# Block means of v beside the first two slots of v by engine copies, beside the others by smaller transfers, in a rearranged order of work

## The chip, the cores and the metric

The kernel runs on one core of a Trainium2 chip. A core has five engines with a queue each: TensorE (PE in the profile; PEld is its weight loads), VectorE (DVE), ScalarE (ACT), GpSimd (POOL) and SyncE (SP), which here only issues transfers. Transfers from every queue share the core's 16 DMA engines. The metric is the time on the device in microseconds, the median of several runs.

## The reference

The kernel computes an attention and behind it two feed-forward layers:

```python
k_sum = k.reshape(B, H, nb, block, D).max(axis=3)      # block = 32
v_sum = v.reshape(B, H, nb, block, D).mean(axis=3)
scores_l = scale * q k^T, kept where |i - j| < 16
scores_s = scale * q k_sum^T + log(block)
a = softmax(concat(scores_l, scores_s))
x = a @ concat(v, v_sum)                                # 1536 tokens x 512
g = relu(x @ w_in) ** 2;            x = g @ w_out       # 512 -> 2048 -> 512
h = x @ w_in2;  g = h * sigmoid(1.702 h);  out = g @ w_out2
```

There are 2 batches, 8 heads, 768 positions and a head size of 64, all in fp32. So each position attends to its near neighbours and to 24 block summaries of its batch.

## The kernel before

**Tiling.** The 1536 tokens are 12 blocks of 128 (`i`, six a batch), 6 units of 256 (`u`), and 3 token tiles of 512. A block is computed in two halves of 64 queries (`c`). Each half attends to a window of 96 neighbouring keys and to the 24 summaries, 120 rows together (`NK`). For the product with v the tile `vw_all` holds, for each of four slots (`NV`, block `i` uses slot `i % 4`) and each half, those 120 rows: the 96 rows of the window come from HBM (`load_vw`, one transfer a half), the 24 rows of the block means come from the tile `vs`.

**The steps.** The string `ORDER` lists them: `k`, `q` load a unit (the last figure tells whether it is packed: one transfer with 512-byte pieces, or two with 256-byte ones), `tk`, `tq` transpose it on PE and copy it out of PSUM, `pk` puts the maxima of k beside the keys of a unit. `sv` (`sum_v`) loads the three v units of a batch into the buffers of k, sums them with a matmul against `band` and copies the means to `vs` in four pieces. `ps` (`put_vs`) puts `vs` into the slots. `v` loads the windows. `h,i,e` (`head`) computes the scores of a block (with `e` 0), and for the four even or odd heads the exponentials on ACT (L559), their sum's small addition on POOL or DVE (L563) and the normalisation (L566). `t,i` (`tail`) transposes the probabilities (L587), copies them to `pT`, multiplies with `vw` (L599: 32 matmuls) and writes the result to `xh` and `xl`, a high and a low part of fp32. `w,f,z` (`prep`, `fetch`) loads a piece of 512 KB of a first-layer weight for one of the 16 slices `f` (z is 0 for `w_in`, 1 for `w_out`) and splits it into parts with ACT (L684, L715) and DVE (L688, L691, L720). `s,f,half` and `S,f` (`part`, `step`) do a slice of the first layer for the first token tile: `S` for all 512 tokens, `s` for 256 of them, so that `s,f,0` needs only the blocks 0 and 1. The products are L753 and L805. Steps of the first layer so begin while attention still runs, and the rest of both layers follows.

**What sets the order.** A planner (`Plan`) takes the steps as the string lists them, gives each operation a start on its engine by fixed costs, and may place a later step in an earlier gap. `soonest` picks the engine that would end first. At the end all instructions are issued in the order of the planned starts, so each engine runs its own list strictly in that order on the chip. Into planned gaps of PE up to the first product L805, `fill` puts matmuls on `ident` (L1108, `warm`) that compute nothing. A transfer issued on POOL (`dma_pool`) is planned to end with a fixed `LAND` after its bytes have moved.

In the kernel before, `put_vs` is two transfers a batch, issued by POOL, one for each half, each copying `vs` into all four slots (L421). Every block's L599 waits for them.

Of the kernel before, what the change touches and what calls it, by code (L numbers as in the profile page):

```python
# [24 lines left out]


ORDER = """
    sel k,1,1 m,0 k,0,1 m,1 k,2,1 tk,0 q,0,1 tk,1 q,1,1 tk,2 pk,2 tq,0 v,0 pk,0 h,1,0 tq,1 m,2 h,1,1 pk,1
    q,3,0 q,2,1 h,0,0 w,1,0 v,1 sv,0 h,3,0 h,0,1 k,3,0 tq,3 ps,0 w,1,1 t,1 h,2,0 v,2 h,2,1 t,0 h,3,1 s,1,0
    v,3 tq,2 tk,3 t,2 h,5,0 t,3 s,1,1 h,4,0 w,3,0 k,4,1 w,3,1 w,5,0 tk,4 s,3,0 w,5,1 s,3,1 w,0,0 k,5,0 S,5  # L30
    w,2,0 tk,5 w,9,0 h,5,1 v,4 pk,3 v,5 h,4,1 pk,4 w,0,1 s,0,0 h,7,0 t,5 w,7,0 w,2,1 s,0,1 sv,1 s,2,0 v,6
    w,9,1 S,9 w,4,0 t,4 w,4,1 s,2,1 h,6,0 q,4,1 w,6,0 S,4 w,6,1 w,7,1 tq,4 S,7 S,6 v,7 w,11,0 w,8,0 ps,1
    w,11,1 h,6,1 h,7,1 h,8,0 S,11 q,5,0 w,8,1 w,10,0 t,7 S,8 w,15,0 v,8 tq,5 h,9,0 t,6 v,9 w,10,1 w,13,0
    w,13,1 S,10 w,15,1 h,8,1 pk,5 w,12,0 t,8 S,13 w,14,0 w,14,1 v,10 h,10,0 S,15 h,9,1 w,12,1 t,9 v,11
    h,11,0 S,14 h,10,1 S,12 h,11,1 t,10 t,11
"""


# [74 lines left out]
class Plan:  # L113
# [8 lines left out]
    ISSUE = 0.5  # L122
    FLIGHT = 1.1
    LAND = 0.95
    lean = 0.5, 0.5

    def __init__(self):
# [19 lines left out]
    def op(self, eng, dur, fn, reads=(), writes=(), after=(), port=False, moves=0.0):  # L147
        ready = self._ready(eng, self._deps(reads, writes, after))
        assert not any(b.dead for b, _ in (*reads, *writes))
        o = Op()  # L150
        o.eng, o.fn, o.seq, o.far = eng, fn, len(self.ops), eng == "SP"
        if eng == "SP":
            o.start = self._place(("SP",), max(ready, 0.8), self.ISSUE)
            self._take("SP", o.start, self.ISSUE)
            t = self._place(("DMA",), o.start + self.FLIGHT, moves)
            if t > o.start + self.FLIGHT:
                self.busy["SP"].remove((o.start, o.start + self.ISSUE))
                o.start = self._place(("SP",), t - self.FLIGHT, self.ISSUE)
                self._take("SP", o.start, self.ISSUE)
                t = self._place(("DMA",), o.start + self.FLIGHT, moves)  # L160
            self._take("DMA", t, moves)
            o.end = t + moves + self.LAND
        else:
            lines = (eng, "PORT") if port else (eng,)
            o.start = self._place(lines, ready, dur)
            for e in lines:
                self._take(e, o.start, dur)
            o.end = o.start + dur
        self.ops.append(o)
        for b, key in reads:  # L170
            b.ops.append(o)
            b.readers.setdefault(key, []).append(o)
        for b, key in writes:
            b.ops.append(o)
            b.writer[key] = o
            b.readers[key] = []
        return o
# [7 lines left out]
    def dma_pool(self, moves, fn, reads=(), writes=()):  # L185

        o = self.op("POOL", 1.0, fn, reads, writes)
        t = self._place(("DMA",), o.end + 0.5, moves)
        self._take("DMA", t, moves)
        o.end, o.far = t + moves + self.LAND, True  # L190
        return o

    def soonest(self, choices, reads=(), writes=(), after=()):
# [61 lines left out]
def kernel(  # L255
# [11 lines left out]
    nc = tc.nc  # L267
    B, H, S, D = q.shape
# [5 lines left out]
    WIN = HALF + 2 * EDGE  # L274
    NSUM = S // BLK
    NK = WIN + NSUM
    NPAIR = H // 2
    NB = S // P
# [11 lines left out]
    NV = 4  # L290
# [13 lines left out]
    plan = Plan()  # L304
# [29 lines left out]
    def make_mask(i):  # L334
        mk = masks[i]
        nc.gpsimd.memset(mk, 0.0)
        for c in range(2):
            w0 = NSUM * (1 - c)
            rows = slice(c * HALF, (c + 1) * HALF)
            part = mk[rows, w0:w0 + WIN]  # L340
            nc.gpsimd.affine_select(out=part, in_=part, pattern=[[1, WIN]], compare_op=ALU.is_ge,
                                    fill=NEG, base=-1, channel_multiplier=-1)
            nc.gpsimd.affine_select(out=part, in_=part, pattern=[[-1, WIN]], compare_op=ALU.is_ge,
                                    fill=NEG, base=2 * EDGE - 1, channel_multiplier=1)
            s0 = 0 if c == 0 else WIN
            nc.gpsimd.memset(mk[rows, s0:s0 + NSUM], LOGB)
        if i == 1:
            nc.gpsimd.memset(mk[0:HALF, NSUM:NSUM + EDGE], NEG)
        if i == 2:
            nc.gpsimd.memset(mk[HALF:P, WIN - EDGE:WIN], NEG)  # L350
# [14 lines left out]
    vw_all = attn.tile([NK, NV, 2, H * D], F32, tag="vw", name="vw")  # L365
    vw_ring = Ring(NV, lambda i: vw_all[:, i])
    vs_of = {}
    vs_rows = [Buf([], None) for _ in range(NV)]
# [5 lines left out]
    kin, qin, qT, kw, ks, vw, vs = {}, {}, {}, {}, {}, {}, {}  # L374
# [39 lines left out]
        vw[i] = buf  # L414

    def put_vs(b):
        for n in range(NV):
            vs_of[n] = b
        for c in range(2):
            r0 = 0 if c == 0 else WIN  # L420
            plan.dma_pool(0.5, lambda c=c, r0=r0: nc.gpsimd.dma_start(  # L421
                out=vw_all[r0:r0 + NSUM, :, c, :], in_=vs[b].t.unsqueeze(1).to_broadcast([NSUM, NV, H * D])),
                reads=[(vs[b], p) for p in range(NPAIR)], writes=[(vs_rows[n], c) for n in range(NV)])

    def sum_v(b):
        ps = banks.take()
# [299 lines left out]
    def prep(m, f, n=None, zs=(0, 1)):  # L726
        for z in zs:
            if z == 0:
                w_sb[m, f] = [None] * 4
            w_sb[m, f][2 * z:2 * z + 2] = hi, lo = [  # L730
                wt.hold() if n is None else wt.named(4 * n + 2 * z + i) for i in range(2)]
            parts(fetch(m, f, z), ALL, hi, ALL, lo, ALL)
# [323 lines left out]
    def part(f, h0, h1):  # L1056
        count = [x + (h0 <= h < h1) for h, x in enumerate(steps)]
        step(0, 0, f, h0 * HT, h1 * HT, [x == 1 for x in count], [x == NF for x in count])
        steps[:] = count

    todo = dict(
        k=load_k, q=load_q, v=load_vw, tk=t_k, tq=t_q,
        h=head, t=tail, ps=put_vs, pk=put_ks, sv=sum_v, w=lambda f, z: prep(0, f, f % RING, (z,)),
        m=lambda i: op("POOL", 1.6, lambda: make_mask(i), writes=[(consts, ("mask", i))]),
        s=lambda f, hf: part(f, hf, hf + 1),
        S=lambda f: part(f, 0, 2),
        sel=lambda: op("POOL", 1.3, make_band, writes=[(consts, "band")]),
# [74 lines left out]
```

## Time and profile before

| | |
|---|---|
| median of 3 runs | 592.22 us (591.78 to 593.14) |
| profiled execution | 593.77 us |
| its span, first to last instruction | 591.8 us |
| PE busy | 572.3 us (97%) |
| DVE busy | 477.4 us (81%) |
| ACT busy | 441.0 us (75%) |
| POOL busy | 65.4 us (11%) |
| moved by DMA | 96.19 MB, 163 GB/s |

Busy time is that of the whole span. It mixes the front, where loads and softmax feed PE, with the long layers behind it, and says little about either. Of use are the stretches of the span, the waits, and the chain of waits that ended last. The profile's line numbers are those of the kernel before; in the changed kernel the lines up to `put_vs` stand 1 further down and those behind it 15.

### The profile page before, as it was taken

The page shows a single profiled execution, that of the slowest core. Times are in us where ns is not written, and L with a number is a line of the kernel's source. Part 1 is how long each engine was busy: PE and PEld are TensorE (multiplying, and loading weights), DVE is VectorE, ACT ScalarE, POOL GpSimd, SP SyncE. Part 2 cuts the span into 40 slices and gives each one's busy share as a digit, 9 for nine tenths or more (in the row PEclk, how much of TensorE's full clock was granted, in tenths as well). Part 3 has the DMA queues.
Part 4 walks back from the last instruction along what each step waited for, and adds up shares of the span by engine and source line. Part 5 has one row for each costly group of instructions (what it writes and reads, how often), then busy time and mean ns, then how long its engine had stood idle before and what let it go on. Part 6 is the DMA issues. An engine that isn't in the chain of part 4 may idle for free.

```text
span 591.8 us, 9749 instructions
## 1 busy us (share of the span) xinstructions
PE 572.3 (97%) x3418; PEld 474.3 (80%) x3418; DVE 477.4 (81%) x1033; ACT 441.0 (75%) x908; POOL 65.4 (11%) x125
## 2 busy tenths in 40 slices
PE   7849999999999999999999999999999999999997
PEld 6648888888888888788888888888878888888885
DVE  4848998888889999889887799899998898877421
ACT  6958988988797768888778876776488777777322
POOL 5123414011200000110000001000100002000000
PEclk9979999999999999999999999999999999999999
DMA  9994999875345552455443536634355555556001
GB/s 227 251 247 101 252 272 237 229 202 171 107 143 178 179 177 73 145 153 182 151 140 119 174 123 207 211 109 140 115 172 161 186 173 164 171 179 210 2 0 72
DMA packets 87633, 96.19 MB, mean 163 GB/s; under 512 B 29536, under 2 KB 74592, under 8 KB 87584
## 3 DMA queue, kind: packets, MB, share of 16 engines
q1 hardware_dynamic: 87264, 94.78, 54.0%
q0 software_dynamic: 320, 0.79, 0.7%
q8 instruction: 27, 0.44, 0.3%
q14 instruction: 22, 0.18, 0.1%
HBM read 91.62 MB, written 3.15 MB: 160 GB/s over the span
## 4 chain that ended last, share of the span: by engine, by line
PE 88%; DMA 4%; DVE 3%; SPq 2%; ACT 1%; issue 1%; POOL 0%; DVEq 0%; POOLq 0%; ACTq 0%
PE acc L805 14%; PE acc L981 13%; PE acc L807 11%; PE m L981 10%; PE m L807 9%; PE h L753 8%; PE m L805 6%; PE acc L753 4%; PE h L981 4%; PE h L807 3%; PE m L753 2%; PE h L805 2%; DMA vw<-vs 2%; PE m L599 1%; DMA kin<-in_v_dram 1%; DMA qin<-in_q_dram 1%
## 5 line engine op out<-in xcount | busy, mean ns | idle before, releaser
L720 DVE TENSOR_TENSOR w<-xw,w 128x512 fp32r<-128x512 f32 (+1 forms) x167 | 111.3, 677 | 6.4 <-ACT w L715 3.5
L715 ACT CAST w<-xw 128x512 fp32r<-128x512 f32 (+1 forms) x164 | 96.9, 601 | 23.1 <-DVE xw L691 16.5
L691 DVE SCALAR_TENSOR_TENSOR xw<-raw,xw 128x512 uint32<-128x512 uint32 x148 | 101.3, 690 | 6.8 <-ACT raw L684 2.5
L684 ACT ACTIVATE raw<-raw 128x512 f32<-128x512 f32 x148 | 96.5, 674 | 9.6 <-DMA raw<-in_moe_w_in_dram 7.1
L805 PE MATMUL acc<-gh,w 128*128 128x512 f32 (+1 forms) x288 | 81.9, 369 | 0.0
L688 DVE TENSOR_SCALAR xw<-raw 128x512 uint32<-128x512 uint32 x148 | 64.0, 437 | 5.8 <-DMA raw<-in_moe_w_out_dram 3.8
L805 PEld LDWEIGHTS acc<-gh,w 128*128 128x128 f32 x288 | 51.7, 188 | 9.1 <-ACT sm L559 0.2
L807 PE MATMUL acc<-w,gh 128*128 128x512 f32 x184 | 56.7, 389 | 0.0
L753 PE MATMUL h<-xh,w 128*128 128x512 f32 (+1 forms) x184 | 55.1, 363 | 0.6 <-DVE r L769 0.5
L805 PE MATMUL acc<-gl,w 128*128 128x512 f32 (+1 forms) x144 | 52.8, 367 | 0.0
L807 PE MATMUL m<-w,gh 128*128 128x512 f32 x156 | 48.2, 390 | 0.0
L981 PE MATMUL acc<-top,w 128*128 128x512 f32 x186 | 47.4, 393 | 0.0
L715 ACT CAST gh<-gs 128x512 fp32r<-128x512 f32 x32 | 19.9, 622 | 35.5 <-PE h L807 25.4
L720 DVE TENSOR_TENSOR gl<-gs,gh 128x512 fp32r<-128x512 f32 x32 | 22.1, 691 | 28.5 <-ACT gh L715 27.9
L981 PEld LDWEIGHTS acc<-top,w 128*128 128x128 f32 x186 | 34.5, 188 | 8.9 <-ACT r L308 1.7
L807 PEld LDWEIGHTS acc<-w,gh 128*128 128x128 f32 x184 | 34.5, 188 | 7.2
L720 POOL TENSOR_TENSOR w<-xw,w 128x512 fp32r<-128x512 f32 x13 | 17.5, 1346 | 194.4 <-ACT w L715 182.5
L753 PEld LDWEIGHTS h<-xh,w 128*128 128x128 f32 x184 | 33.1, 188 | 6.5 <-DVE r L769 0.8
L559 ACT ACTIVATE sm<-sm,st 128x120 f32<-128x120 f32 x96 | 36.6, 383 | 0.0
L807 PE MATMUL acc<-w,gl 128*128 128x512 f32 x92 | 35.8, 389 | 0.0
L981 PE MATMUL m<-top,w 128*128 128x512 f32 x138 | 35.3, 391 | 0.0
L807 PEld LDWEIGHTS m<-w,gh 128*128 128x128 f32 x156 | 29.2, 188 | 6.3 <-ACT gh L782 0.4
(191 smaller groups left out, 1219.0 us busy)
## 6 DMA issues: line engine op xcount, KB each, us to landing
raw<-in_moe_w_out_dram SPq DMA_DIRECT2D x88, 512.0 KB, 3.5
raw<-in_moe_w_in_dram SPq DMA_DIRECT2D x60, 512.0 KB, 3.9
vw<-in_v_dram SPq DMA_DIRECT2D x20, 192.0 KB, 5.8
kin<-in_v_dram SPq DMA_DIRECT2D x6, 512.0 KB, 7.1
out_dram<-r SPq DMA_DIRECT2D x12, 256.0 KB, 2.1
kin<-in_k_dram SPq DMA_DIRECT2D x4, 512.0 KB, 6.1
qin<-in_q_dram SPq DMA_DIRECT2D x4, 512.0 KB, 7.2
qin<-in_q_dram SPq DMA_DIRECT2D x4, 256.0 KB, 4.8
```

The costliest lines, as they stand in the source:

```text
L559: nc.scalar.activation(out=s.t[:, h, :], in_=s.t[:, h, :], func=AF.Exp, bias=st.t[:, 0, h:h + 1], scale=-1.0, accum_out=st.t[:, 1, h:h + 1])
L599: nc.tensor.matmul(ps.t[e * D:(e + 1) * D, p * P + c * HALF:p * P + (c + 1) * HALF], lhsT=vw[i].t[:, c, h * D:(h + 1) * D], rhs=t.t[:, h, ...
L684: nc.scalar.activation(out=top, in_=top, func=AF.Prelu, scale=-(2.0 ** -80), alpha=-(2.0 ** -32))
L688: op("DVE", 0.36, lambda: nc.vector.tensor_scalar(out=x.t, in0=raw.t[:, :, 0], scalar1=29, scalar2=None, op0=ALU.logical_shift_right), rea ...
L691: op("DVE", 0.64, lambda: nc.vector.scalar_tensor_tensor(out=x.t, in0=raw.t[:, :, 1], scalar=3, in1=x.t, op0=ALU.logical_shift_left, op1=A ...
L715: plan.soonest([("ACT", 0.09 + 0.44 * fr, False, lambda: nc.scalar.copy(out=hi.t[:, hc], in_=src())), ("DVE", 0.05 + 0.4 * fr, True, lambd ...
L720: eng.tensor_tensor(out=lo.t[:, lc], in0=src(), in1=hi.t[:, hc].bitcast(F32), op=ALU.subtract)
L753: nc.tensor.matmul(hp.t[:, cols], lhsT=w.t[:, kc * P:(kc + 1) * P], rhs=x.t[:, kc, cols], start=(kc == 0 and n == 0), stop=(kc == KC - 1 a ...
L805: nc.tensor.matmul(a.t[:, cols], lhsT=w.t[:, j * P:(j + 1) * P], rhs=g.t[:, cols], **st)
L807: nc.tensor.matmul(a.t, lhsT=g.t[:, j * P:(j + 1) * P], rhs=w.t, **st)
L981: nc.tensor.matmul(bank.t, lhsT=a, rhs=rhs(b, kh), start=(begin and k == 0 and n == 0), stop=(k == 1 and n == 2), skip_group_check=True)
```

## The change

For each batch `put_vs` now does two things. For the first two slots that the batch uses (`near`: slots 0 and 1 in the first batch, 2 and 3 in the second) it copies `vs` with an engine, slot by slot and half by half, so four copies of 24x512, each on whichever of POOL, ACT and DVE the planner finds free soonest. For the other two slots POOL issues two transfers of half the size. In the plan a transfer of POOL is now taken to end 4 us later (`BEHIND`). And `ORDER` is another list, with the same steps.

```diff
 ORDER = """
-    sel k,1,1 m,0 k,0,1 m,1 k,2,1 tk,0 q,0,1 tk,1 q,1,1 tk,2 pk,2 tq,0 v,0 pk,0 h,1,0 tq,1 m,2 h,1,1 pk,1
+    m,1 k,2,1 sel w,1,0 m,0 k,1,1 q,1,1 k,0,1 tk,0 tk,1 tk,2 pk,0 q,0,1 sv,0 tq,0 h,1,0 tq,1 m,2 h,1,1 h,0,0
...
     LAND = 0.95
+    BEHIND = 4.0
...
-        o.end, o.far = t + moves + self.LAND, True
+        o.end, o.far = t + moves + self.LAND + self.BEHIND, True
...
     def put_vs(b):
+        near = (b * NB) % NV
+        for n in (near, near + 1):
+            for c in range(2):
+                r0 = 0 if c == 0 else WIN
+
+                def go(eng, n=n, c=c, r0=r0):
+                    (eng.copy if eng is nc.scalar else eng.tensor_copy)(
+                        out=vw_all[r0:r0 + NSUM, n, c, :], in_=vs[b].t)
+
+                plan.soonest([("POOL", 1.1, True, lambda go=go: go(nc.gpsimd)),
+                              ("ACT", 0.6, False, lambda go=go: go(nc.scalar)),
+                              ("DVE", 0.5, True, lambda go=go: go(nc.vector))],
+                             reads=[(vs[b], p) for p in range(NPAIR)], writes=[(vs_rows[n], c)])
+        far = NV - 2 - near
+        for c in range(2):
+            r0 = 0 if c == 0 else WIN
+            plan.dma_pool(0.6, lambda c=c, r0=r0: nc.gpsimd.dma_start(
+                out=vw_all[r0:r0 + NSUM, far:far + 2, c, :], in_=vs[b].t.unsqueeze(1).to_broadcast([NSUM, 2, H * D])),
+                reads=[(vs[b], p) for p in range(NPAIR)], writes=[(vs_rows[n], c) for n in (far, far + 1)])
         for n in range(NV):
             vs_of[n] = b
-        for c in range(2):
-            r0 = 0 if c == 0 else WIN
-            plan.dma_pool(0.5, lambda c=c, r0=r0: nc.gpsimd.dma_start(
-                out=vw_all[r0:r0 + NSUM, :, c, :], in_=vs[b].t.unsqueeze(1).to_broadcast([NSUM, NV, H * D])),
-                reads=[(vs[b], p) for p in range(NPAIR)], writes=[(vs_rows[n], c) for n in range(NV)])
```

What this moves is seen in three lists. The first is SP's, whose transfers start in this order, near the start of the program. In the kernel before, from its fourth load on (`qin` a q unit, `kin` a k unit, or a v unit where it is read from `in_v_dram`, `vw` a window of v, `raw` a weight piece; `x2` two alike):

```order
L380 DMA qin_152<-in_q_dram 128x8x128
L380 DMA qin_173<-in_q_dram 128x8x128
L411 DMA vw<-in_v_dram 80x8x64
L411 DMA vw<-in_v_dram 96x8x64
L386 DMA qin_240<-in_q_dram 128x8x64 x2
L380 DMA qin_300<-in_q_dram 128x8x128
L675 DMA raw_340<-in_moe_w_in_dram 128x4x256
L411 DMA vw<-in_v_dram 96x8x64 x2
L429 DMA kin_382<-in_v_dram 128x8x128
L429 DMA kin_422<-in_v_dram 128x8x128
L429 DMA kin_439<-in_v_dram 128x8x128
```

and in the changed one from its second load on:

```order
L690 DMA raw_107<-in_moe_w_in_dram 128x4x256
L381 DMA kin_128<-in_k_dram 128x8x128
L381 DMA qin_164<-in_q_dram 128x8x128
L381 DMA kin_179<-in_k_dram 128x8x128
L381 DMA qin_205<-in_q_dram 128x8x128
L444 DMA kin_219<-in_v_dram 128x8x128
L444 DMA kin_236<-in_v_dram 128x8x128
L444 DMA kin_267<-in_v_dram 128x8x128
L694 DMA raw_288<-in_moe_w_out_dram 128x1024
L387 DMA qin_321<-in_q_dram 128x8x64 x2
L412 DMA vw<-in_v_dram 80x8x64
```

The three v units for the means moved ahead of two q units and of all windows of v, and two weight pieces moved ahead of the windows.

The second list is ACT's, around the copies to `vs` (`sm` and `st` are the softmax of a block, `ACTIVATE` of them its exponentials, `pT` transposed probabilities, `xh` the result of a block). In the kernel before:

```order
L308 COPY pT1_480<-acc1_457 120x4x128
L308 COPY pT1_480<-m0_483 120x4x128
L308 COPY qT1_502<-acc1_489 64x512
L308 COPY vs0_517<-acc2_442 24x128 x3
L559 ACTIVATE sm0_495,st0_496<-sm0_495,st0_496 128x120 x8
L559 ACTIVATE sm2_429,st2_430<-sm2_429,st2_430 128x120 x4
L308 COPY kw3_150<-m2_539 128x4x128
L308 COPY kw3_150<-acc2_548 128x4x128
L684 ACTIVATE raw1_554<-raw1_554 128x512
L308 CAST xh0_619<-acc0_575 128x4x128
```

and in the changed one:

```order
L309 COPY vs0_356<-m2_269 24x128 x3
L574 ACTIVATE sm0_331,st0_332<-sm0_331,st0_332 128x120 x8
L574 ACTIVATE sm1_388,st1_389<-sm1_388,st1_389 128x120 x4
L699 ACTIVATE raw1_288<-raw1_288 128x512
L574 ACTIVATE sm1_388,st1_389<-sm1_388,st1_389 128x120 x4
L730 CAST w6_463<-xw1_421 128x512
L424 COPY vw_75<-vs0_356 24x512
L309 COPY qT0_473<-acc2_412 128x512
L309 COPY qT0_473<-m2_423 128x512
L574 ACTIVATE sm2_477,st2_478<-sm2_477,st2_478 128x120 x4
L309 COPY pT0_513<-m0_442 120x4x128
L309 COPY pT1_537<-acc0_515 120x4x128
```

Before, three halves of the softmax come behind the copies to `vs` and five ahead of them; now all halves come behind them, and a copy to `vw` stands among them.

The third is PE's list around the first two products with `vw`. Before, they are the rows that read `pT0_394` and `pT1_480`:

```order
L458 MATMUL m2_539<-ident_70,kin0_469 128x128 x4
L458 MATMUL acc2_548<-ident_70,kin0_469 128x128 x4
L1108 MATMUL warm_87<-ident_70 128x128 x3
L587 MATMUL m1_569<-ident_70,sm0_495 120x128 x4
L599 MATMUL acc0_575<-pT0_394,vw_75 64x64 x16
L599 MATMUL h0_600<-pT1_480,vw_75 64x64 x16
L587 MATMUL acc1_626<-ident_70,sm0_495 120x128 x4
```

and after, those that read `pT0_513` and `pT1_537`:

```order
L602 MATMUL acc0_515<-ident_70,sm1_388 120x128 x4
L602 MATMUL acc1_528<-ident_70,sm1_388 120x128 x4
L614 MATMUL m1_540<-pT0_513,vw_75 64x64 x16
L614 MATMUL h0_564<-pT1_537,vw_75 64x64 x16
L602 MATMUL acc1_590<-ident_70,sm2_477 120x128 x4
L1123 MATMUL warm_100<-ident_70 128x128 x3
L768 MATMUL h0_610<-xh0_581,w4_181 128x256
```

Before, a unit of k and a half of a third block's probabilities are transposed ahead of these products, and a head and more transposes stand between them and the first half-step (`xh`, `w`); now the half-step follows them after one transposition.

## Rows read from the trace of the kernel before

**Rows 1.** Stretches of the span: us, busy time of each engine (instructions), granted clock, DMA share, GB/s.

```profile
0.00:34.90 34.90, 26.71 (x317) 22.55 (x318) 23.20 (x101) 28.14 (x89) 12.91 (x57) 1.00 1.06 238
34.90:48.44 13.54, 7.29 (x112) 6.25 (x110) 5.60 (x14) 5.17 (x13) 2.32 (x6) 0.62 0.89 208
48.44:84.00 35.56, 34.27 (x406) 30.81 (x405) 32.22 (x100) 32.12 (x91) 11.16 (x20) 1.00 0.82 209
84.00:588.00 504.00, 504.00 (x2591) 414.71 (x2589) 416.38 (x821) 374.93 (x717) 38.96 (x42) 1.00 0.49 152
```

**Rows 2.** Waits of PE up to 48 us: engine, line, waited for: total, times, longest.

```profile
PE acc L599 <- DMA vw<-vs: 6.3, 2, 5.7
```

**Rows 3.** PE in order of time: start, us, line, operation, what ended its idle time.

```profile
5.02 1.09 PE L458 MATMUL acc<-ident,kin 128*128 128x128 f32 x4 [0.23 <-DMA kin<-in_k_dram]
...
12.47 0.63 PE L458 MATMUL acc<-ident,qin 128*128 128x128 f32 x4 [0.72 <-DMA qin<-in_q_dram]
...
48.44 0.36 PE L753 MATMUL h<-xh,w 128*128 128x256 f32 x1
```

**Rows 4.** The chain that ended last, 0 to 50 us: start, us, what.

```profile
29.18 0.68 PE acc L437 x16
...
31.33 0.81 POOL vw L421
32.14 9.75 DMA vw<-vs
...
41.94 1.76 PE acc L599 x28
```

**Rows 5.** The same chain later, at full clock.

```profile
51.90 1.53 ACT sm L559 x8
...
91.43 1.08 PE m L599 x32
...
101.19 0.87 PE m L458 x8
...
112.95 0.98 PE m L536 x32
...
119.65 0.87 PE m L587 x8
```

**Rows 6.** Groups by line: engine, operation, shapes, count, busy us, mean ns, idle before.

```profile
L684 ACT ACTIVATE raw<-raw 128x512 f32<-128x512 f32 x148 | 96.5, 674 | 9.6 <-DMA raw<-in_moe_w_in_dram 7.1 <-DMA raw<-in_moe_w_out_dram 2.5
...
L720 POOL TENSOR_TENSOR w<-xw,w 128x512 fp32r<-128x512 f32 x13 | 17.5, 1346 | 194.4 <-ACT w L715 182.5 <-ACT raw L684 6.6 <-PE m L599 5.3
...
L308 ACT COPY pT<-m 120x512 f32<-120x512 f32 x17 | 9.7, 583 | 1.9 <-PE m L587 1.9
...
L612 DVE TENSOR_TENSOR xl<-m,xh 128x512 fp32r<-128x512 f32 x9 | 6.2, 689 | 4.5 <-ACT xh L308 4.5
...
L308 ACT COPY vs<-m 24x128 f32<-24x128 f32 x4 | 1.0, 258 | 0.5 <-PE m L437 0.5
```

**Rows 7.** Shorter stretches, the columns of rows 1.

```profile
0.00:3.00 3.00, 1.57 (x7) 1.57 (x8) 0.00 (x0) 1.28 (x1) 2.00 (x14) 1.00 0.14 38
...
12.00:15.00 3.00, 1.90 (x14) 1.54 (x14) 2.37 (x7) 2.93 (x5) 0.87 (x6) 1.00 1.32 206
...
45.20:54.00 8.80, 8.80 (x160) 7.85 (x162) 6.34 (x25) 6.76 (x20) 1.83 (x5) 0.90 0.12 30
54.00:84.00 30.00, 28.71 (x302) 25.58 (x295) 28.94 (x83) 26.78 (x75) 9.74 (x17) 1.00 0.97 248
```

**Rows 8.** Transfers that read `vs`, issue to landing; one DVE operation, ns min/median/max.

```profile
DMA to landing us min/median/max: 8.5/9.2/9.8
...
L688 DVE TENSOR_SCALAR xw<-raw x148: 397/420/1516, 23.5 to 544.0; 128x512 uint32<-128x512 uint32 x148
```

**Rows 9.** The page's DMA issues: what, queue, count, KB each, us to landing.

```profile
vw<-in_v_dram SPq DMA_DIRECT2D x20, 192.0 KB, 5.8
kin<-in_v_dram SPq DMA_DIRECT2D x6, 512.0 KB, 7.1
```

More of the change, by code (lines that the diff above doesn't have):

```diff
@@ L27 @@
 ORDER = """
-    sel k,1,1 m,0 k,0,1 m,1 k,2,1 tk,0 q,0,1 tk,1 q,1,1 tk,2 pk,2 tq,0 v,0 pk,0 h,1,0 tq,1 m,2 h,1,1 pk,1
[L29 to L35, printed above, removed]
+    m,1 k,2,1 sel w,1,0 m,0 k,1,1 q,1,1 k,0,1 tk,0 tk,1 tk,2 pk,0 q,0,1 sv,0 tq,0 h,1,0 tq,1 m,2 h,1,1 h,0,0
+    w,1,1 pk,1 q,2,0 v,0 h,0,1 ps,0 h,3,0 tq,2 v,1 t,1 h,2,0 v,2 v,3 pk,2 h,2,1 t,0 h,3,1 k,3,0 t,2 s,1,0
+    t,3 tk,3 w,2,0 q,3,0 tq,3 k,4,1 tk,4 w,3,0 h,4,0 s,1,1 w,3,1 h,5,0 s,3,0 k,5,0 s,3,1 w,5,0 h,5,1 w,2,1
+    w,0,0 q,4,1 s,2,0 tk,5 w,5,1 S,5 w,9,0 s,2,1 w,6,0 h,4,1 pk,3 w,9,1 v,4 S,9 w,6,1 pk,5 tq,4 w,0,1 t,4
+    v,5 h,7,0 w,7,0 s,0,0 t,5 w,7,1 s,0,1 w,4,0 S,7 q,5,1 w,11,0 pk,4 w,4,1 h,6,0 sv,1 S,4 h,7,1 v,6 ps,1
+    w,8,0 w,11,1 tq,5 v,7 t,7 S,6 h,6,1 w,10,0 h,8,0 v,8 S,11 h,9,0 h,8,1 t,6 w,8,1 h,9,1 v,9 v,10 w,15,0
+    t,8 S,8 w,10,1 S,10 w,12,0 w,12,1 w,15,1 v,11 t,9 h,10,0 w,13,0 S,12 S,15 w,14,0 h,11,0 w,13,1 h,10,1
+    S,13 w,14,1 h,11,1 t,10 S,14 t,11
 """
```

## The prediction

> **What bounds the kernel now.** I read first the stretches of the span, to find where TensorE (PE) loses time. From 84.00 to 588.00 us PE is busy 504.00 of 504.00 us at full clock, so nothing there can be won by moving work, and the 3.8 us behind it are the last copy and store. From 48.44, where the first half-step of the first layer starts [rows 3], to 84.00 PE idles 35.56 - 34.27 = 1.3 us. All other loss lies ahead of 48.44: 34.90 - 26.71 = 8.2 us of idle in the first stretch and 13.54 - 7.29 = 6.3 us in the second, which also runs at a mean granted clock of 0.62 [rows 1]. So the end is set by two things only: when the first half-step starts, and how much useful PE work is already done by then. The total PE work is the same in both kernels, since the instruction lists differ in warm-up matmuls alone.
>
> Next I asked what PE waits for ahead of 48.44. One entry is 6.3 us in two waits, the longer 5.7 us: the first attention-times-v product (L599) waits for the transfer of the block means `vs` into `vw` [rows 2]. The chain of waits shows the place: the transfer is issued at 31.33 on GpSimd (POOL), which takes 0.81, and is then under way 9.75 us, until 41.9; after it the 28 matmuls that are left of the first product take 1.76 us [rows 4], against 1.08 us for all 32 at full clock [rows 5]. That is PE at 1.2 GHz, the lower of its two levels, after standing idle since about 35.2. Stall and low clock are one loss: the work between 34.90 and 48.44 would need at full clock two products (2.16), four groups of four softmax transposes (1.74) and a head (0.98), about 4.9 us by [rows 5], against the 13.54 us that it took. So 8.7 us is what a perfect repair of this place would give.
>
> **The change part by part.** *The copies.* For the first two `vw` slots of a batch, four copies of 24x512 replace the transfer. In the first batch DVE makes two, ScalarE (ACT) one, POOL one. No row shows this shape. From below, a copy of a quarter of the columns (24x128) takes 0.258 us on ACT; from above, a 120x512 one takes 0.583 [rows 6]. I take 0.58 on ACT, the row with as many columns. On DVE I take the 0.42 of its 128x512 op that reads and writes SBUF [rows 8]. POOL's lies between nothing and the 1.35 us of its two-input 128x512 op [rows 6]; it runs while the softmax is computed and costs nothing as long as that lasts. Only ACT's 0.58 is on the path below. In the second batch the same four copies lie where PE has no idle at all, and the wait there was already zero [rows 1]: I cost them and the later start at nothing, as PE's queued work hides them.
>
> *The small transfers.* The other two slots get two transfers of half the bytes, issued on POOL between the small additions of the softmax. Each issue costs POOL between 0 and 0.81 us [rows 4]; the additions behind it wait so long, but the first two come at least 1.5 us (one softmax half, [rows 5]) ahead of the last one that counts. A landing of 8.5 to 9.8 us [rows 8] from about 25 us ends near 35.
>
> *The order of loads.* Before, the v units for the means came as loads fourteen to sixteen, behind three k units, five transfers of q, a weight half and four slices of v for `vw`; now they are loads seven to nine, behind three k, two q and one weight half, all of one size, 512 KB [rows 9]. The first five such loads of the kernel before are there at 5.02 to 12.47 us, by the transposes that wait for them, or 1.86 us apart [rows 3]; the ninth lands at 5.02 + 8 x 1.86 = 19.9. Checked by rate: nine times 0.524 MB at the 238 GB/s of the first stretch [rows 1] is 19.8 us.
>
> *The path to the first half-step.* ACT now has its part of the copies to `vs` in its queue ahead of all exponentials, so the ninth load holds everything up. 19.9, sum over v 0.68 (20.6), three copies to `vs` 0.78 (21.4), four softmax halves of 1.53 each, a half being the exponentials of four heads of a block (27.5), one weight pass 0.67 (28.2), then a weight cast, the `vw` copy and two q copies at 0.58 (30.5), the fifth half 1.53 (32.0), one copy of transposed probabilities 0.58 (32.6): the first product can start [rows 4 to 6]. The windows of v that it needs are no later: one weight half at 238 GB/s, then q unit 2 and four slices of at most 192 KB (together 1.31 MB, [rows 9]) at the 206 GB/s of the stretch in which the first such slices move [rows 7] are there at 19.9 + 2.2 + 6.4 = 28.5. The two products, 1.08 each, end at 33.7 and 34.8; behind the first stand one copy on ACT (0.58, 34.3) and then three steps of 0.69 on DVE, the last for the second product, done at 36.4 [rows 6]. The half-step starts at 36.4 instead of 48.44, 12.0 us earlier.
>
> *What is not done by then.* The PE list of the change has, ahead of the first half-step, 16 fewer transposes of k and q (1.74), 12 fewer of the softmax (1.31) and one head fewer (0.98), 4.0 us [rows 5], and they have to be done later. So the shift is worth 12.0 - 4.0 = 8.0 us.
>
> *What is late next.* The loads. Between 45.20 and 54.00 the kernel before moves 30 GB/s, an idle of the queues that the earlier start takes away; from 54 to 84 it runs at 248 GB/s with a DMA share of 0.97 [rows 7]. Up to 84.00 it moved 34.9 x 238 + 13.54 x 208 + 35.56 x 209 = 18.6 MB [rows 1]. At 248 GB/s from about 2.5 us on (in the first 3 us hardly anything moves, [rows 7]) that takes until 77.3, so a shift by more than 84.0 - 77.3 = 6.7 us needs the data sooner than the queues bring it, except for what was loaded ahead of its use (three buffers of 512 KB, 6.3 us). I take 6.7, and 0.5 off it for loads that now arrive just in time: k unit 3 lands at 19.9 + 2.2 + 2.62 MB at 206 GB/s = 34.8, and it, q unit 3 and k unit 4 are each wanted within about 3 us of landing. **Sum: 6.2 us gained**, 593.77 - 6.2 = 587.6 for the profiled execution, which was 1.55 us above the median of its runs, 592.22; for the median 586.0.
>
> **A rule that speaks against it.** At 31.33 POOL issues its transfers beside DVE ops that read PSUM; the issue took 0.81 [rows 4]. The change puts two DVE copies from SBUF to SBUF next to such issues, and no row shows that pair; the nearest is a DVE op whose slowest took 1.516 us where the median is 0.420 [rows 8]. The Trainium skill, "SBUF — State Buffer", section "SBUF: two separate sides", says that an fp32 copy on DVE within SBUF locks GpSimd out of the port pair they share, so that it cannot write the descriptors of its own DMA. By that rule the second issue, and the addition behind it, would come one DVE copy later, 0.42 us, and the sum would be 5.8 us (586.4); with the slowest op as the price, 1.1 us, 5.1 (587.1). No run here shows it yet.
>
> **The rivals.** *The wait moves to the loads.* For it: the queues are at a share of 0.97 whenever PE is fed from them [rows 7], and the eleven loads behind the ninth are mostly of the kind that ran at 206 GB/s. Against it: three buffers of look-ahead. If the look-ahead is already used up and the rate of 206 holds for the 18.6 MB's slow third, the shift shrinks by 6.2 MB x (1/0.206 - 1/0.248) = 5.1 us, and 1.2 to 4 us remain: 588.2 to 591.0. *The wait moves to the small transfers.* The second pair of slots is wanted at about 38 to 40; by the row of 9.8 us they are there at 35, and they would have to land past 39 to hold PE. For every us beyond it PE stands still. The Trainium skill, "DMA: Bandwidth & Descriptors", section "Anatomy of one DMA — SWDGE (gpsimd) path", fits 2.0 us plus the bytes at 436 GB/s, 2.45 us for 192 KB; the trace has 9.75, so the measurement decides and I plan with it. I count this with the first rival, at the same times. *Nothing comes of it.* The chain of DVE and ACT from 48 to 84, where both are busy about 32.2 of 35.56 us [rows 1], would be the bound, and the copies and the second order take back the rest: 591.0 to 593.4. *Slower.* One mechanism: the ninth load now gates all exponentials. If the v units land no earlier than before (the last at 29.2 us, where PE's sum over v starts [rows 4]), the half-step starts 9.3 us after 36.4, at 45.7, with 4.0 us of work still to do: 45.7 + 4.0 - 48.44 = 1.3 us slower, 593.5, and up to 596 if the loads are then late too. It decides from a landing at 19.9 + 8.0 = 27.9 on. *More.* If look-ahead hides the whole lack of loads and the softmax runs with fewer gaps than summed, the gain is the 8.7 us of a perfect repair and up to 1 us of the 8.2 us idle ahead of it: 582.5 to 583.2, from 9 us on.
>
> **How the numbers follow.** Forecast (a gain of 4 to 9 us, 583.2 to 588.2) 0.66, with 586.0 in it; the waits moved (588.2 to 591.0) 0.15; nothing 0.07; slower 0.07; more 0.05. About 0.2%, 1.2 us, is what a measurement of this kernel can tell from no change. The forecast, the moved waits and the larger gain are faster by more than that: 0.86; the same 0.07; slower 0.07. The range has to leave out no more than 2 in 10: 583.0 to 590.8 leaves out the two cases without a gain, most of the larger gain and a little of the moved waits.
>
> **What would show each step.** Right: in the profile after, no wait of L599 on the transfer from `vs`; the first product at 32 to 33 us, the first half-step (L753, now L768) at 36 to 37; a granted clock near 1.00 from 30 to 50 us; no trough of 30 GB/s near 45 to 54; PE without idle from about 78 on. Wrong: the sum over v ending past 22 us (the order of loads mis-sized), PE idle on k or q loads between 36 and 50 (the loads are the new wait), a wait of L599 on the small transfers near 39, or PE idle anywhere in the last 500 us, which I hold for unchanged.

## The result, and the profile after

The changed kernel takes 586.67 us (median of 4 runs, 586.42 to 587.40) against 592.38 us of the kernel before beside it (4 runs, 591.78 to 593.14): a ratio of 0.9905, 95% interval 0.9888 to 0.9922, some 5.7 us faster. Measured again with the last experiments it took 586.88 us (6 runs, 586.26 to 587.16), ratio 0.9912 (0.9893 to 0.9930). Its profiled execution took 586.43 us, its span is 584.6 us: 7.2 us less than the 591.8 before. The two profiled executions differ by more than the medians do, because before's lay 1.4 us above its median and after's at the bottom of its runs.

The stretches of the kernel after, with the columns of [rows 1], the last boundary now at 580.00:

```profile
0.00:34.90 34.90, 27.64 (x384) 24.28 (x385) 24.36 (x102) 26.11 (x75) 13.95 (x57) 1.00 1.07 234
34.90:48.44 13.54, 12.84 (x192) 11.54 (x195) 11.91 (x23) 12.89 (x39) 4.67 (x13) 1.00 0.98 265
48.44:84.00 35.56, 34.68 (x301) 30.99 (x291) 32.91 (x105) 32.84 (x91) 8.31 (x14) 1.00 0.86 241
84.00:580.00 496.00, 495.76 (x2577) 407.35 (x2576) 411.19 (x813) 368.75 (x706) 38.86 (x42) 1.00 0.48 150
```

The second line is the change: PE is busy 12.84 of 13.54 us at full clock, where [rows 1] has 7.29 at a granted clock of 0.62. PE's busy share in the other lines hardly moved. PE in order of time, the answers to [rows 3] and [rows 4]: the last part of the sum over v, the first product, the first half-step.

```profile
19.16 0.64 PE L452 MATMUL m<-kin,band 128*24 128x128 f32 x16
...
32.20 1.15 PE L614 MATMUL m<-pT,vw 120*64 120x64 f32 x32
...
36.18 0.35 PE L768 MATMUL h<-xh,w 128*128 128x256 f32 x1 [0.62 <-DVE st L588]
```

The first product waits for nothing any more, and the half-step starts 12.3 us earlier than the 48.44 of [rows 3]. The span gains only 7.2 of those 12.3 us, because less work is done by the half-step (some 5.0 us, reckoned below). What the 7.2 us consist of can be read from PE's busy time. Matmuls on `ident` that compute nothing (`warm`) cost PE 10.2 us before and now 12.2. First the line of the kernel before, then of after, from the groups by line:

```profile
L1108 PE MATMUL warm<-ident 128*128 128x128 f32 x58 | 10.2, 315 | 1.4 <-POOL ident masks.py:199 1.4
```

```profile
L1123 PE MATMUL warm<-ident 128*128 128x128 f32 x80 | 12.2, 305 | 1.4 <-POOL ident masks.py:199 1.4
```

With the page's busy times (572.3 and 571.6 us) the spans part exactly. Before: 562.1 us of useful work, 10.2 warm, 19.5 idle (the tail included). After: 559.4 useful, 12.2 warm, 13.0 idle. So idle fell by 6.5 us, 2.0 of the time so freed went to warm-up matmuls, and useful work takes 2.7 us less because none of it runs at the low clock: 6.5 - 2.0 + 2.7 = 7.2.

### The profile page after: what moved, and what is told of

It is laid out like the page before. It is cut to its first block, busy times and chain, and to the rows that moved or that the text cites. A ratio compares the mean times of both kernels' runs of the same rounds, so it can differ in the third digit from the quotient of the medians.

```text
span 584.6 us, 9824 instructions
## 1 busy us (share of the span) xinstructions
PE 571.6 (98%) x3440; PEld 474.3 (81%) x3440; DVE 480.4 (82%) x1040; ACT 441.8 (76%) x909; POOL 65.8 (11%) x125
## 4 chain that ended last, share of the span: by engine, by line
PE 86%; ACT 5%; DVE 4%; DMA 3%; SPq 1%; issue 1%; POOL 0%; DVEq 0%; ACTq 0%
PE acc L996 13%; PE acc L820 13%; PE acc L822 11%; PE m L996 10%; PE m L822 9%; PE h L768 6%; PE m L820 6%; PE h L996 3%; PE acc L768 3%; PE m L768 3%; PE h L822 3%; PE h L820 2%; ACT sm L574 2%; PE m L614 2%; DMA kin<-in_k_dram 1%; DMA kin<-in_v_dram 1%
## 5 line engine op out<-in xcount | busy, mean ns | idle before, releaser
L735 DVE TENSOR_TENSOR w<-xw,w 128x512 fp32r<-128x512 f32 (+1 forms) x163 | 107.5, 672 | 5.9 <-ACT w L730 4.0
L703 DVE TENSOR_SCALAR xw<-raw 128x512 uint32<-128x512 uint32 x148 | 65.8, 449 | 6.2 <-DMA raw<-in_moe_w_out_dram 5.8
L822 PE MATMUL acc<-w,gh 128*128 128x512 f32 x192 | 59.1, 389 | 0.0
L822 PE MATMUL m<-w,gh 128*128 128x512 f32 x148 | 45.7, 390 | 0.0
L730 ACT CAST gh<-gs 128x512 fp32r<-128x512 f32 x32 | 19.9, 622 | 33.5 <-PE acc L822 25.4
L735 POOL TENSOR_TENSOR w<-xw,w 128x512 fp32r<-128x512 f32 x17 | 22.9, 1344 | 195.9 <-ACT w L730 170.2
L996 PEld LDWEIGHTS acc<-top,w 128*128 128x128 f32 x192 | 35.8, 188 | 8.5 <-ACT r L309 1.2
L822 PEld LDWEIGHTS acc<-w,gh 128*128 128x128 f32 x192 | 36.0, 188 | 7.5
L822 PE MATMUL acc<-w,gl 128*128 128x512 f32 x96 | 37.4, 389 | 0.0
L996 PE MATMUL acc<-xh,w 128*128 128x512 f32 x100 | 34.0, 389 | 0.0
```

The source lines that it names most:

```text
L703: op("DVE", 0.36, lambda: nc.vector.tensor_scalar(out=x.t, in0=raw.t[:, :, 0], scalar1=29, scalar2=None, op0=ALU.logical_shift_right), rea ...
L730: plan.soonest([("ACT", 0.09 + 0.44 * fr, False, lambda: nc.scalar.copy(out=hi.t[:, hc], in_=src())), ("DVE", 0.05 + 0.4 * fr, True, lambd ...
L735: eng.tensor_tensor(out=lo.t[:, lc], in0=src(), in1=hi.t[:, hc].bitcast(F32), op=ALU.subtract)
L822: nc.tensor.matmul(a.t, lhsT=g.t[:, j * P:(j + 1) * P], rhs=w.t, **st)
L996: nc.tensor.matmul(bank.t, lhsT=a, rhs=rhs(b, kh), start=(begin and k == 0 and n == 0), stop=(k == 1 and n == 2), skip_group_check=True)
```

## The experiments

Each ran in five rounds beside the kernel before (medians of before: 592.39 us for the first four, 592.08 for the next four, 591.70 for the last three). Ratios are to that, with their 95% interval.

### The copies alone

The lists of the kernel before stay as they are; POOL makes two copies ahead of its transfers, now of half the size, and ACT two behind its last copy to `vs`.

```diff
 def put_vs(b):               # POOL's place of the first transfer
+    if c == 0: two copies of vs on POOL into the near slots
-    dma vs -> vw_all[r0:r0 + NSUM, all four slots, c]
+    dma vs -> vw_all[r0:r0 + NSUM, far:far + 2, c]
 last copy to vs on ACT
+    two copies of vs on ACT into the near slots
```

> The kernel before with its lists of instructions as they were; only, in each batch, ACT makes two of the four copies to the first two slots right behind its last copy to vs, POOL makes the other two ahead of its transfers, and the transfers carry the other two slots alone. Theory (the end goes with the first half-step, and that waits for the means in vw or for the softmax, whichever is later; the order of loads is one of two ways to the same gain): the first product no longer waits for a transfer but for the third block's normalisation ahead of it on PE, so it starts at 35 to 36.5 us instead of 40.9, PE stays at full clock, and the first half-step starts at 41 to 43 instead of 48.4: 5 to 7 us faster than before, about 586. Rival 'the order does it': within 1.2 us of before. Rival 'the copies do it all': 5.7 us faster or more.

Measured: 587.99 us (587.54 to 588.89), ratio 0.9929 (0.9913 to 0.9946). In the trace the last part of the sum over v is nearly where it was, at 28.61 us (29.18 before), but the first product runs at 35.26 us instead of 41.94 [rows 4], the half-step starts at 40.81 instead of 48.44, and PE idles 0.9 us from 34.90 to 48.44:

```profile
35.26 1.15 PE L620 MATMUL acc<-pT,vw 120*64 120x64 f32 x32
...
40.81 0.39 PE L774 MATMUL h<-xh,w 128*128 128x256 f32 x1 [0.57 <-DVE xl L633]
```

So the copies alone bring most of the gain, 4.4 us, though less than the 5 to 7 expected; the product came when the theory said, the half-step a little earlier (41 to 43 expected).

### The order alone

The lists of the change; the copies are left out and each transfer fills all four slots again.

```diff
-                def go(eng): copy vs -> vw_all[r0:r0 + NSUM, n, c, :]
+                def go(eng): pass
-                out=vw_all[r0:r0 + NSUM, far:far + 2, c, :]
+                out=vw_all[r0:r0 + NSUM, :, c, :]
```

> The changed kernel with its lists as they are, without the engine copies; the transfers of each batch, issued at the same places, carry vs into all four slots, as before the change. Theory: the transfers are issued at 22.9 and 24.4 us and land 9.2 to 9.8 us later, the second at about 34; the first product starts then instead of at 32.2, and the end is 1.5 to 2.5 us later than the change's: about 588.5, still 3 to 4 us faster than before. Rival 'the order does it': the same time as the change, 586.7. Rival 'the copies do it': back to 592.

The two lists differ in one thing besides their order: q unit 2 is no longer packed and q unit 5 is, so that the transposes of unit 2 leave PSUM in two copies of 128x512 instead of four of 64x512. "Order" below includes this; its share was not run apart.

Measured: 587.11 us (586.39 to 588.77), ratio 0.9915 (0.9897 to 0.9933), not to be told from the change. The transfers are issued at 23.9 and 25.1 us instead of 31.3, and the second lands while the first product runs. Its only wait on them, from PE's waits between 30 and 36 us:

```profile
PE m L613 <- DMA vw<-vs: 0.5, 1, 0.5
```

So the theory that without copies the large transfers would hold the product for long was wrong. The two halves of the change are two remedies for one wait, and the gains do not add: 4.4 us by the copies, 5.3 by the order, 4.8 to 5.7 by both.

### The wait kept, the clock held

The kernel before with 24 matmuls on `ident` (48 instructions in the profile) ahead of the first product, which fill the wait.

```diff
         def pv():
+            for _ in range(24 if i == 1 else 0):
+                keep_warm()
```

> The kernel before with 24 more matmuls on ident ahead of the first product, which compute nothing and fill PE's wait of 5.7 us; all else as before. It parts the wait from the low clock behind it. Theory: the product starts no earlier (about 41), but PE is then at full clock, and what took 7.5 us from 40.9 to the first half-step takes 4.5 to 5.5: 2 to 3 us faster than before, 589 to 590. Rival 'ACT and DVE set the pace there, the clock costs nothing': within 0.5 us of before.

Measured: 590.31 us (589.55 to 591.77, 12 runs), ratio 0.9968 (0.9956 to 0.9980), 2.1 us less than before. The stretch that ran at 0.62 [rows 1] in this kernel:

```profile
34.90:48.44 13.54, 13.54 (x234) 12.89 (x234) 7.05 (x26) 8.27 (x20) 2.71 (x7) 1.00 0.88 210
```

PE is busy all the time at full clock, and the split of the span is 559.2 useful, 15.7 warm, 13.4 idle: the useful work is as short as in the change, and the wait itself, now filled with warm-up, is still there. One thing more differs in this execution: the transfers landed 7.4 to 7.7 us after their issue, in the kernel before 9.6 to 9.8, so the first product ran from 40.56 us, where before four of its matmuls ran at 40.94 and the rest from 41.94. The half-step started at 44.99, 3.45 us earlier than before, and about 1.4 of these come with the earlier landing. From 40.56 to the half-step it is 4.43 us, from 41.94 in the kernel before 6.50. So the low clock was worth 2 to 3 us of the loss (2.1 by this distance, 2.9 by the useful work, 562.1 - 559.2) and the wait the rest. How long the wait is in those executions of the kernel before that were not profiled is not known.

### More to load ahead, and behind

A load of 448 KB into a buffer that nothing reads, in the change: once just ahead of the v units, once just ahead of k's fifth unit, which comes behind all that the first half-step needs.

```diff
+    nc.sync.dma_start(out=spare..., in_=q[1, 0:7, 0:UNIT, :]...)   # 448 KB
     plan.dma(1.85, lambda: nc.sync.dma_start(   # v unit 0, or k unit 4
```

> The changed kernel with one more load, 448 KB of q into a spare buffer that nobody reads, ahead of the three v units; all else as it is. Theory (the ninth load gates the exponentials, and the half-step and the end with them): the sum over v ends 1.6 to 1.9 us later, so do the first product and the first half-step, and the end is 1.2 to 1.9 us later than the change's, about 588.2. Rival 'the exponentials have slack': 0 to 0.5 us later.

Ahead: 587.89 us (587.24 to 589.69), ratio 0.9931 (0.9913 to 0.9950), 1.2 us by medians above the change as first measured, 1.0 above the second measurement; the intervals overlap in part. That is about the lower end of what the theory says and more than the rival's. The profiled execution took 589.69 us, with a granted clock of 0.86 from 20 to 30 us, and the last part of its sum over v began 2.9 us later than in the change, so only distances in it are used: from the last part of the sum to the half-step it is 17.39 us, in the change 17.02. So the half-step follows the sum.

> The change with one more load, 448 KB of q into a buffer that nothing reads, just ahead of the load of k's fifth unit: some 1.8 us of the queues at the 248 GB/s of 54 to 84 us, behind everything that the first half-step needs. By the step of the prediction that capped the gain at 6.7 us because the queues must still bring what lies ahead of 84 us, the time should rise by 1.2 to 1.8 us. By the rival, that the loads run far enough ahead of the engines, it rises by 0 to 0.5 us and no new wait of TensorE on a load shows after 36 us.

Behind: 587.27 us (586.80 to 588.67), ratio 0.9923 (0.9907 to 0.9939), 0.4 to 0.6 us above the change by medians, less than the intervals can tell. Two of the six runs took 588.6 and 588.7 us, the other four 586.8 to 587.3, and the trace is of one of the two (588.58). In the change no wait on a load is among PE's waits from 36 to 84 us; here, in the same view, there is one:

```profile
PE m L481 <- DMA kin<-in_k_dram: 1.1, 2, 0.7
```

So in this execution 1.1 of the 1.8 us that the extra load takes reach PE, and its span is 2.2 us above that of the change, of which 0.5 lie ahead of the half-step (36.64). In the other four the time rose by some 0.6 us at most; whether they had the wait is not known. By medians the rival holds, in the trace the wait that it excluded is there: the loads were not the bound in the change, and less than 1.8 us away from being it.

### A copy moved off ScalarE, twice

In the kernel after, the chain to the first product runs over the fourth copy:

```profile
27.80 0.63 ACT w L730
28.44 0.62 ACT vw L424
29.08 0.59 ACT qT L309
```

The first kernel has POOL make that copy, behind its second transfer.

```diff
+                if b == 0 and o.eng == "ACT":
+                    o.fn = lambda: None        # and the copy behind POOL's second transfer
```

> The lists of the change, with one instruction moved: the fourth block-mean copy of batch 0, which ACT makes at 28.44 us (0.62 us) between a weight cast and a copy of qT, is made by POOL behind its second transfer instead (POOL stands idle there from 25.05 to 25.65 us). The chain of the kernel after runs through that ACT copy, on to the qT copy, the scores and the first product at 32.20 us, so the first product and the first half-step should come 0.6 us earlier (31.6 and 35.6 us), and the time should fall by 0.3 to 0.6 us (theory: what the change still loses sits on ACT ahead of 36 us). Rival: POOL's own chain (a softmax product of 1.52 us from 28.47 us) or VectorE binds right behind, and nothing moves (0 to 0.2 us).

Measured: 588.41 us (587.12 to 589.00), ratio 0.9931 (0.9915 to 0.9947): slower than the change, 1.5 us by medians, and the span is 586.8. Both expectations fell. The trace shows why. POOL and then DVE in this kernel, in order of time:

```profile
25.30 1.11 POOL L425 COPY vw<-vs 24x512 f32<-24x512 f32 x1
...
29.02 0.99 POOL L593 TENSOR_TENSOR sm<-sm,st 128x480 f32<-128x480 f32 x1 [0.30 <-DVE st L600]
```

```profile
25.29 0.66 DVE L593 TENSOR_TENSOR sm<-sm,st 128x480 f32<-128x480 f32 x1 [0.51 <-ACT sm L586]
25.98 0.72 DVE L425 COPY vw<-vs 24x512 f32<-24x512 f32 x1
...
29.04 1.52 DVE L747 TENSOR_TENSOR w<-xw,w 128x512 fp32r<-128x512 f32 x1
```

POOL's copy takes 0.60 us in the change and 1.11 here, beside a DVE product that began 0.01 us earlier; DVE's copy, 0.41 to 0.42 alone, starts while POOL still copies and takes 0.72. The later pair shows it best: here POOL starts first and takes 0.99, DVE starts 0.02 us later and takes 1.52. In the kernel after the same pair stands the other way round, DVE first. POOL's line and DVE's line there:

```profile
28.47 1.52 POOL L581 TENSOR_TENSOR sm<-sm,st 128x480 f32<-128x480 f32 x1 [0.30 <-DVE st L588]
```

```profile
28.45 0.69 DVE L735 TENSOR_TENSOR w<-xw,w 128x512 fp32r<-128x512 f32 x1
```

Whoever starts second is held up until the other is nearly done. A shift of some hundredths of a us so took 0.53 us off POOL, which had room, and put 0.83 us on DVE, which computes the masked scores next; PE's first product came at 32.88 instead of 32.20 and the half-step at 37.32 instead of 36.18; 0.22 of this lies already in the sum over v (19.38, in the change 19.16). That these places make up all of the 1.5 us is not shown: at 76.13 us PE waits another 1.22 us for a softmax product of DVE, a wait that the change has not, and what holds that product up was not followed. The Trainium skill, "SBUF — State Buffer", section "Who interferes with whom", says that a DVE operation with two SBUF inputs and a GpSimd operation that reads SBUF exclude each other for the whole instruction, and that the order of issue decides who waits. The rows agree but for 0.14 us: the second takes 0.85 and 0.55 us beyond the end of the first, where it takes 0.99 and 0.69 when it goes first.

The second kernel puts the copy into DVE's gap of 0.51 us ahead of its second softmax product.

```diff
+                if b == 0 and o.eng == "ACT":
+                    o.fn = lambda go=go: go(nc.vector); moved.append(o)
...
+        moved[0].start = 24.95
```

> The lists of the change with ACT's block-mean copy of batch 0 made by VectorE in the gap of 0.51 us in which it waits for ACT's exponentials (24.57 to 25.08 us in the kernel after; such a copy takes 0.41 us), while POOL only issues a transfer. The run that moved the same copy to POOL came out later, with a POOL copy of 1.11 us beside a VectorE product of two operands and a VectorE copy of 0.72 us behind it. Theory: the two engines take turns, and the place was the fault, not the move: here the copy takes 0.41 us, the first product comes 0.4 to 0.6 us earlier than in the change (31.6 to 31.8 us), and the time falls by 0.2 to 0.6 us. Rival: that run's loss came from ACT's list without the copy, and this one is 1 to 2 us above the change as well.

Measured: 586.56 us (586.12 to 587.48), ratio 0.9910 (0.9891 to 0.9929), against 0.9912 of the change in the same rounds: the same. In this profiled execution the clock was 0.79 between 12 and 20 us, and the sum over v ends 1.0 us later than in the change, so distances count: from the last part of the sum to the first product 12.55 us instead of 13.04, to the first half-step 16.89 instead of 17.02. The copy costs nothing in the gap, the product gains the 0.5 us expected, and the half-step keeps 0.1 of it. So the loss of the POOL version was the place, not ACT's shorter list.

### The weight split moved behind

The same, and the splitting of one weight half put behind the exponentials and the qT copies on ACT, and behind the masked scores on DVE; five planned warm-up matmuls are left out, as the wait that they fill gets shorter.

```diff
+        at = {95: 29.9, 97: 30.0, 98: 33.3, 99: 33.66}   # ACT scale, DVE, ACT cast, DVE difference
+        for n, t in at.items():
+            plan.ops[n].start = t
```

> The same, and the split of one half of the second weight block (ACT scale 0.59 us, VectorE 0.69 us, ACT cast 0.62 us, VectorE difference 0.69 us), which stands between the exponentials and the qT copies, put behind them, with half of the matmuls that keep the clock left out there since TensorE needs not wait so long. In the kernel after, that split lies on the chain to the first product at ACT 25.56 and 27.80 us, and its last step is what POOL's softmax product of 1.52 us at 28.47 us shares its time with. Theory: the first product comes at 30.4 to 31.0 us and the first half-step at 34.4 to 35.2 us, 1.0 to 1.8 us earlier than in the change; the loads had some 0.7 us to spare by the run with one more load, so the time falls by 0.7 to 1.5 us. Rival: the weights of the first half-step then come last (the cast and the difference end at 33 us or later), or VectorE and ACT, which have 43.6 and 44.5 us of work in the 47.8 us from 36.2 to 84 us, give it back: within 0.4 us of the change.

Measured: 586.94 us (586.12 to 588.01), ratio 0.9913 (0.9891 to 0.9935): the same as the change. From the last part of the sum over v (20.25 us here) the first product comes after 11.99 us, 1.05 earlier than in the change, but the half-step after 17.03, as in the change. PE in order of time:

```profile
32.24 1.15 PE L619 MATMUL m<-pT,vw 120*64 120x64 f32 x32
...
37.28 0.36 PE L773 MATMUL h<-xh,w 128*128 128x256 f32 x1 [1.70 <-DVE st L593]
```

The half-step waits 1.70 us for DVE, against 0.62 in the change: the rival held. The gain is given back on DVE: the weight difference that was moved behind (0.68 us at 33.71) now stands there between the product and the half-step, the greater part of the 1.05 us. No version found beats the change.

### No transfers, and a plan with measured prices

Each transfer replaced in its place by two copies on POOL:

```diff
-            plan.dma_pool(0.6, lambda c=c, r0=r0: nc.gpsimd.dma_start(...))
+            plan.dma_pool(0.6, both, ...)      # two nc.gpsimd.tensor_copy
```

> The lists of the change; each of the two transfers of a batch is replaced, in its place on POOL, by two block-mean copies (2 x 0.60 us instead of an issue of 0.63 to 0.80 us). Theory: what counts is that the rows stand before the first product and the later ones before theirs, and both do, so the time stays within 0.5 us of the change. Rival (the port that POOL and VectorE share, or POOL's four small operations of the softmax, which stand behind these places, delayed by 0.4 to 0.6 us each): the softmax of the third half comes later, the first half-step at 36.5 to 37.3 us, and the time is 0.4 to 1.1 us above the change.

Measured: 588.40 us (587.54 to 588.85), ratio 0.9932 (0.9916 to 0.9948); the half-step starts at 37.70 us. The rival held, and the loss is larger than it said: 1.5 to 1.7 us above the change by medians, where 0.4 to 1.1 was expected. Two POOL copies at 23.20 us take 1.58 us where 1.20 was counted, DVE's softmax products beside these and the next two 0.83 and 1.00 us instead of 0.66.

And the change replanned with POOL at 0.6 us a copy instead of 1.1, DVE at 0.4, and ACT no choice:

```diff
-                plan.soonest([("POOL", 1.1, ...), ("ACT", 0.6, ...), ("DVE", 0.5, ...)],
+                plan.soonest([("POOL", 0.6, ...), ("DVE", 0.4, ...)],
```

> The change replanned with the measured prices: POOL 0.6 us a copy instead of 1.1, VectorE 0.4, and ACT no choice. The planner then puts the products of the first two tiles earlier by four places and moves one load of q on SP. If the chain over ACT's copy is what is left to gain, 0.5 to 1.0 us below the change; if the order list was fitted to the old prices, the new one is no better or up to 1.5 us worse.

Measured: 589.67 us (589.36 to 590.28), ratio 0.9957 (0.9941 to 0.9974): half of the gain is gone, 2.8 to 3.0 us by medians, more than the worse of the two expectations. The new list starts the first half-step at 42.10 us and has 13.8 us of warm-up. The price of 1.1 need not be an error of the planner: it is about what a POOL copy took beside a DVE product (1.11 above). But the list differs in many places, so how much of the loss is the price is open.

The 4 us of `BEHIND` were not run without: with 0 in its place the lists of all five engines are the same, instruction for instruction. That part of the change does nothing here.

## Why the prediction came out right, step by step

**The place of the loss** held. The whole gain lies ahead of 84 us, the wait of L599 is gone, the clock is 1.00 from 30 to 50 us. One sign named as right failed, by little: PE was to have no idle from 78 us on, and it has 0.50 us at 82.04 and 0.24 between 84 and 580. The perfect repair of 8.7 us held wait and low clock together; the run with warm-up in the wait shows the low clock at 2 to 3 us.

**The order of loads** was mis-sized by little: the ninth load was counted at 19.9 us, and PE's sum over its data begins at 19.16.

**The path to the half-step** came out almost as summed: product at 32.20 (32.6 counted), half-step at 36.18 (36.4). The copies cost 0.62 on ACT (0.58 counted), 0.41 on DVE (0.42) and 0.60 on POOL (0 to 1.35). That the ACT copy is on the path is shown by its removal: the product comes 0.5 us earlier. That its removal shortens the time was not said and is not so: DVE is next.

**The small transfers** were priced with the landing of the large ones, 8.5 to 9.8 us [rows 8], and took less. The transfers that read `vs`, in the kernel after:

```profile
DMA to landing us min/median/max: 5.1/5.5/5.8
```

They landed near 30 us, ten ahead of need; it decided nothing. A landing of some 7 us at the new place, as in the run without copies, is also why the old transfer would almost have done.

**What is not done by the half-step** was the first term that failed: 4.0 us counted, 5.0 measured. Up to the half-step useful busy time was 26.71 - 10.17 + 7.29 = 23.8 us before, less 2.7 lost to the clock, 21.1, and is 28.30 - 12.23 = 16.1 after. The instruction counts were right (28 transposes and a head). The price was that of back-to-back groups of eight [rows 5], while the missing ones stand mostly in groups of four, 0.60 to 0.65 us each in the timelines, which overlap their neighbours in part; that this is the whole of the 1.0 us is likely and not shown. So the shift was worth 12.3 - 5.0 = 7.3, not 8.0.

**The loads as the next bound** was the second term that failed: the cap of 6.7 and the 0.5 for just-in-time loads took 1.8 us off. In the change PE waits for no load after 36 us and the span fell by 7.2, more than the cap allows. The rate in the cap was right: the changed kernel moves 249 GB/s from 2.5 to 76.8 us (84.0 less 7.2), where 248 was reckoned, and the trough of 30 GB/s [rows 7] is gone, as forecast. At that rate the 18.6 MB are there at about 77 us, as reckoned (77.3). What failed is the step from full queues to a PE that waits for them: ACT waits 1.4 us for weight pieces from 36 to 84 us and DVE 0.2, and none of it reaches PE as a wait on a load. The run with one more load shows that the bound is near, less than 1.8 us away.

**The sum.** The two errors had opposite signs for the gain, 0.7 us too much and 1.8 too little, so 6.2 was forecast for the profiled execution and 7.3 came: that the two partly cancel is luck. The medians moved by 5.7 and 4.8 us. That the forecast median lies within 0.7 us is so in part owed to a third cancelling: the difference of the profiled execution to the median, 1.55 us, was carried over to the changed kernel, whose profiled execution lay at its fastest run.

**The rule on the port** (the Trainium skill, "SBUF — State Buffer", section "SBUF: two separate sides") was weighed at the wrong instructions. For a DVE copy beside the issue of a transfer it would have cost 0.42 us. In the first batch of the change no DVE copy to `vw` stands beside an issue. The kernels with the copy in DVE's gap have the pair, POOL's line first and DVE's second:

```profile
25.58 0.72 POOL L439 DMA_DIRECT2D vw<-vs  x1
```

```profile
25.77 0.42 DVE L426 COPY vw<-vs 24x512 f32<-24x512 f32 x1
```

The issue took 0.72 us instead of 0.63 and ended 0.11 us behind the copy, so it took 0.09 us more and not 0.42. In the second batch of the change a DVE copy (0.41 us, from 97.96 us) lies across the two issues, which together take 1.41 us from 97.40; in the run of the order alone, without copies, they take 1.25. Dearer are POOL's own operations on data beside DVE's. The first batch of the change has two such places: POOL's small addition at 27.73 us takes 0.44 us instead of 0.21 to 0.23 beside a DVE copy that began at 27.68, and its product at 28.47 takes 1.52.

**The rivals.** Waiting loads: not in the change, though less than 1.8 us away. Nothing and slower: refuted, since the sum over v came 10 us earlier and the half-step 12. Not among the rivals was the one that the experiments found: that either half of the change would have done most of it. The prediction put the gain to both together and gave neither a price of its own.

## What to carry to other kernels

Where a change holds two remedies for one wait, price each alone; here either gives over three quarters of the gain and the second adds at most 1.3 us by medians. When a start moves earlier, count what is done by then in busy time, with filler matmuls taken off, rather than by instruction counts at their best price. An engine copy that replaces a transfer has to be placed against what VectorE and GpSimd do at that moment: the same copy was free on DVE in a gap (0.42 us), and on POOL beside a two-input operation it took 1.11 us instead of 0.60, in a kernel that was 1.5 us slower.

## What the runs showed of the hardware

The exclusion of POOL and DVE down to the single pair (POOL 0.99 and DVE 1.52 us, or DVE 0.69 and POOL 1.52, by who starts first) was not expected in this strength. And the landing of the transfers from `vs` goes by neither size nor place alone. Half the size landed 1.0 to 1.8 us sooner at the new place (5.1 to 5.8 us against 6.1 to 7.6 without copies) but hardly sooner at the old one (7.2 to 7.6 with copies in the old lists, 7.4 to 7.7 for the full size in the run with warm-up), and the same full-size transfers took 9.6 to 9.8 us at the same place in the kernel before. What makes that difference of 2 us, in lists that differ in PE's warm-up alone, stays open.
